# A fused attention and routed feed-forward kernel: another order of work at the start, and three output products behind the last P V

## The chip, the cores and the metric

The kernel runs on one core of one Trainium2 chip. The time is the device time of one execution in microseconds (us), taken as the median of three runs. Five engines work side by side and wait for each other by semaphores: TensorE (in a profile PE, and PEld for its weight loads), VectorE (DVE), ScalarE (ACT), GpSimd (POOL) and SyncE (SP), which here only issues DMAs. Each engine takes its instructions in the order in which they were written.

## The reference: what is computed

With x of 2048 rows and 512 columns, in float32:

```python
g = sigmoid((x * gate_w).sum(-1, keepdims=True))
# a: attention, 32 heads of 16, softmax over all 2048 keys, then wo
q, k, v = split(x @ wqkv)
a = merge(softmax(q @ k.T * 16 ** -0.5) @ v) @ wo
# b: two rows of x, those with the largest r, get a gated feed-forward
r = x @ w_r
idx = argsort(-r)[:2]
y = (silu(x[idx] @ w_gate) * (x[idx] @ w_up)) @ w_down
b = x, with y * sigmoid(r[idx]) added to the rows idx
return g * a + (1 - g) * b
```

## The kernel before, in words

The heads are taken in 16 pairs. A pair has two units of 1024 queries, 32 units in all, and a unit is 16 steps of 128 keys: 512 steps. A step has four score matmuls (`s_piece`, L648) with an exp each on ScalarE (L649) and, two steps later, the P V product (`av_mm`, L657). So that the exp can't overflow, the negative row maxima of the scores are found ahead, by a second product of the same queries and keys (`m_piece`, L576) and a reduction on VectorE (L580). Float32 operands go through TensorE as a high and a low half. `split` makes the halves (high on ScalarE, L70 or L73; low on VectorE, L71 or L74), and the three products of halves are summed. `pool_split` (L77, L78) does the same on GpSimd.

The order is written by hand. `ORDER` (L31) gives the order of pieces for three steps: s is a score piece, m a maximum piece, A a P V, f a piece of other work out of the generator `slots` (projections of the other groups, the feed-forward, the output product with wo). `at_step` hangs small tasks behind a step; `late` holds tasks until the next turn of the loop. Functions in `gaps` are run on VectorE between two reductions.

**The start.** Warm-up products run while weights (`load_w`, L118) and x (`load_x`, L138, four blocks of 512 rows) are loaded. x and the weights of head group 0 are split. `proj` (L146) makes one block of k or q out of twelve products in a PSUM bank (three banks with the tag "st", shared with V's parts and the score pieces). The block is split on leaving the bank; `first_rows` copies its rows for pair 0 into `Kx[0]` or `Qx[0]`, four DMAs a block (L202, L203), and `store_ev` (L176) puts the whole block into DRAM, from where later pairs load it. The blocks leave through two buffers with the tag "ev" (even blocks) or through the tiles Qx[1] and Qx[2] (odd blocks). Before the lead stand k0, q0, k1, k2, k3 and four parts of three products of q1.

**The lead.** `LEAD` is 21 steps of maximum pieces alone (`m_lead`, L607, reduced at L612): 16 for unit 0 and five for unit 1. Between them TensorE takes parts of three products from `lead_parts`: q1, q2, q3, and 64 parts of V (`v_part`, L283), three parts a step, four in the first four steps. Parts that are left come at the first two A of the loop. The first lead step reads blocks 0 and 1 of K, from the fifth on blocks 2 and 3 as well. At the same time the router's and the gate's products of x run on GpSimd (`products`, L315), with their sums on ScalarE (`sums`, L319); the rows of x for them come by `load_rows` (L307, L309). After the last lead step a transpose (`r_row`, L331) turns the router's sums into rows.

**Queues.** All DMAs but the indirect ones are issued by SyncE, in program order. A DMA waits there until the one issued eight before it has landed, and for its data.

**The end.** Once the maxima are done the loop becomes one step at a time: four score pieces, a P V, one piece of `slots`. The last pieces are `wo_last` (L554): the product of head group 3 with wo for one block of 128 rows, three matmuls (L498), added into `acc` on VectorE (`finish`, L549) and stored (`store`, L552). Blocks 8 to 11 come from step 505 on. `tail` (L740) takes the last unit, which covers rows 1536 to 2047: it copies o out of PSUM (L670), sums and inverts the denominators (L746, L748), spreads them (L751, L752, L755), scales o (L758), splits it and makes four output blocks (L765), each finished and stored.

Of the kernel before, what the change touches and what calls it, by code (L numbers as in the profile page):

```python
# [8 lines left out]
F32 = mybir.dt.float32  # L9
# [27 lines left out]
def gated_mix(ctx: ExitStack, tc: tile.TileContext, xT, x, wqkv, wo, w_rg, w_gate, w_up, w_down,  # L37
# [74 lines left out]
    def load_w(g):  # L112
        ws = ring.tile([128, 2, 4, 128], F32, tag="w", name="ws", bufs=3)
        W[g] = ws
        for i in (1, 0):
            if g == 0 and i == 0:
                load_x(0)
            nc.sync.dma_start(ws[:, i], ap(wqkv, i * D + g * 128, [[3 * D, 128], [128 * 3 * D, 4], [1, 128]]))  # L118

    def split_w(g, parts=(1, 0)):  # L120
        if 1 in parts:
# [24 lines left out]
    def proj(g, which, nb, piece):  # L146
        i = "qk".index(which)
        wh, wl = W[g]
        ps = fl_tile() if g else st_tile()
        n = 0  # L150
        for terms in (((wh, xh), (wl, xh)), ((wh, xl),)):
            for c in range(4):
                for a, b in terms:
                    nc.tensor.matmul(ps, a[:, i, c, :], b[nb][:, c, :], start=n == 0, stop=n == 11)  # L154
                    n += 1
                    if n % piece == 0 and n < 12:
                        yield
        if g:
            if (g, which, nb) == (2, "q", 3):
                late.append((split_w, (3, (1,))))  # L160
                at_step(now[0] + 2, split_w, 3, (0,))
            late.append((evict, (g, which, nb, ps)))
            yield
            return
        if nb % 2:
            ev = Qx[1 if nb == 3 else 2].rearrange("p (a n) -> p a n", a=2)
        else:
            ev = ring.tile([128, 2, 512], F32R, tag="ev", name="ev", bufs=2)
        scale = 0.25 if which == "q" else 1.0
        split(ev[:, 0], ev[:, 1], ps, scale=scale)  # L170
        first_rows(which, nb, ev)
        store_ev(0, which, nb, ev)
        yield

    def store_ev(g, which, nb, ev):
        nc.sync.dma_start(  # L176
# [17 lines left out]
    def first_rows(which, nb, ev):  # L194

        if which == "q" and nb > 1:
            return
        t = (Kx if which == "k" else Qx)[0][:, nb * 512:nb * 512 + 512].bitcast(F32)
        for j in range(2):
            e = ev[16 * j:16 * j + 16].bitcast(F32)  # L200
            two = e if which == "k" else e[:, 0:1, :].to_broadcast([16, 2, 512])
            nc.sync.dma_start(t[64 * j:64 * j + 32], two)  # L202
            nc.sync.dma_start(t[64 * j + 32:64 * j + 48], e[:, 0 if which == "k" else 1, :])  # L203

    def proj0(which, nb):
        for _ in proj(0, which, nb, 12):
# [7 lines left out]
    load_w(0)  # L214
    for nb in range(1, 4):
        load_x(nb)
    nc.sync.dma_start(cst, consts)
    wvs = ring.tile([128, 4, 512], F32, tag="P", name="wvs", bufs=3)
    nc.sync.dma_start(wvs, ap(wqkv, 2 * D, [[3 * D, 128], [128 * 3 * D, 4], [1, D]]))
    def ones(k):  # L220
        for j in range(2):
            nc.gpsimd.memset(k[64 * j + 32:64 * j + 64, :].bitcast(F32), 1.0)
# [9 lines left out]
    split_x(2)  # L232
    proj0("q", 0)
    split_x(3)
    for nb in (1, 2, 3):
        proj0("k", nb)
    wv = [wvs, Kx[1].rearrange("p (c n) -> p c n", c=4),
          ring.tile([128, 4, 512], F32R, tag="P", name="wvl", bufs=3)]
    for c in range(4):
# [47 lines left out]
    def lead_parts():  # L287

        v = [(t, c) for t in range(KT) for c in range(4)]
        yield from proj(0, "q", 1, 3)  # L290
        for n in range(8):
            v_part(*v.pop(0))
            yield
        for nb in (2, 3):
            yield from proj(0, "q", nb, 3)
        while v:
            v_part(*v.pop(0))
            yield
# [4 lines left out]
    def load_rows(nb):  # L303
        if nb == 0:
            rg["w"] = o_tile("wr", [128, D]), o_tile("wg", [128, D])
            for i in range(2):
                nc.sync.dma_start(rg["w"][i], ap(w_rg, i * D, [[0, 128], [1, D]]))  # L307
        t = ring.tile([128, 4, D], F32, tag="xs", name="xn", bufs=2)
        nc.sync.dma_start(t, ap(x, nb * 512 * D, [[D, 128], [128 * D, 4], [1, D]]))  # L309
        rg[nb] = t  # L310

# [17 lines left out]
    def r_row():  # L329
        ps = fl_tile((16, 128))  # L330
        nc.tensor.transpose(ps, gz[:, :, 0], ident)  # L331
        rg["row"] = ring.tile([16, 128], F32, tag="rt", name="rt", bufs=1)
        nc.scalar.activation(rg["row"], ps, AF.Copy)

    def route_rows():

# [403 lines left out]
    def tail():  # L740
        u = UNITS - 1
        hl = [o_tile(n, [128, 512], F32R) for n in ("onh", "onl")]
        o = AV[u]
        ps = st_tile((128, 16))
        for c in range(4):
            nc.tensor.matmul(ps[:, 4 * c:4 * c + 4], o[:, c * 128:c * 128 + 128], sel_l, start=True, stop=True)  # L746
        r = ring.tile([128, 16], F32, tag="r16", name="rl", bufs=2)
# [2 lines left out]
        rb = r[:, :, None].to_broadcast([128, 16, 32])  # L750
        nc.scalar.activation(rx[:, 0:8], rb[:, 0:8], AF.Copy)  # L751
        nc.vector.tensor_copy(rx[:, 8:16], rb[:, 8:16])  # L752
        pr = [mxb_tile((128, 256)), fl_tile((128, 256))]
        for c in range(4):
            nc.tensor.matmul(pr[c // 2][:, c % 2 * 128:c % 2 * 128 + 128],  # L755
# [3 lines left out]
        for t in range(2):  # L759
            sl = slice(256 * t, 256 * t + 256)  # L760
            split(hl[0][:, sl], hl[1][:, sl], o[:, sl])
        banks = [st_tile(), mxa_tile()[:, 0], st_tile(), mxb_tile()]
        for t in range(4):
            for n, (a, b) in enumerate(((0, 0), (1, 0), (0, 1))):
                nc.tensor.matmul(banks[t], hl[a][:, t * 128:t * 128 + 128], wz[0][:, b, :], start=n == 0, stop=n == 2)  # L765
# [21 lines left out]
    at_step(1, gates, 0)  # L787
    at_step(2, gaps.append, lambda: nc.vector.max(top8, rg["row"]))
    at_step(3, gaps.append, route_rows)
    at_step(4, gaps.append, partial(gates, 1))  # L790
    at_step(10, gaps.append, lambda: nc.vector.max(best8, cand))
    at_step(12, gaps.append, route_best)
    at_step(18, route_index)
    at_step(22, route_gate, 0)
    at_step(24, gather)
    at_step(27, gaps.append, partial(route_gate, 1))
    at_step(-8, load_w, 1)
    at_step(-5, split_w, 1)
    at_step(2, load_w, 2)
# [11 lines left out]
    def slots():  # L811
# [110 lines left out]

    while count["m"] < UNITS * EL:
        run_late()
        for o in ORDER:
# [60 lines left out]
```

## Time and profile before

| | us |
|---|---|
| median of three runs | 1433.41 (1433.03 to 1433.73) |
| the profiled execution, its own time | 1430.75 |
| its span, first to last instruction | 1428.9 |
| mean granted TensorE clock | 0.999 |

The profile is that of one execution. A row of the timeline gives start, length, engine (SPq is SyncE's issue of a DMA), line, operation and what it writes and reads; in brackets stands how long the engine had been idle and what ended that. PE and PEld overlap, and matmuls are pipelined. A row "x9" merges nine instructions.

### The profile page before, as it was taken

What the parts mean: (1) busy time and instruction counts of PE and PEld (TensorE: products, weight loads), DVE (VectorE), ACT (ScalarE), POOL (GpSimd) and SP (SyncE); (2) the same over time, 40 slices, a digit from 0 to 9 for tenths busy, and PEclk for the clock granted to TensorE, in tenths of its full rate; (3) what the DMA queues carried; (4) which work ended last, traced back from release to release, by engine and by line L of the source; (5) the groups of instructions that cost most, each with busy time, mean ns of one, the idle gap of its engine ahead of it and who ended that gap; (6) DMA issues with size and microseconds to landing.
All of it is one profiled execution on the core that took longest, in us unless ns stands there. A gap on an engine that the chain in (4) does not pass through costs nothing.

```text
span 1428.9 us, 24152 instructions
## 1 busy us (share of the span) xinstructions
PE 1417.6 (99%) x9113; PEld 628.9 (44%) x9113; DVE 1292.6 (90%) x1534; ACT 1169.4 (82%) x2262; POOL 312.9 (22%) x329
## 2 busy tenths in 40 slices
PE   9999999999999999999999999999999999999998
PEld 6654444444444444444444443434444444444433
DVE  5879999999999999999999999999999999999942
ACT  4468888888888888888888888888888888888886
POOL 3661100112000001200000100032742322234500
PEclk9999999999999999999999999999999999999999
DMA  8611021212214121312222332414313031012012
GB/s 261 183 56 49 20 53 31 54 45 43 53 52 109 62 53 31 68 29 57 65 82 53 85 84 77 106 41 134 83 31 68 21 77 35 15 31 58 17 50 78
DMA packets 55096, 92.87 MB, mean 65 GB/s; under 512 B 14208, under 2 KB 25472, under 8 KB 53476
## 3 DMA queue, kind: packets, MB, share of 16 engines
q1 hardware_dynamic: 54884, 91.32, 24.7%
q8 instruction: 72, 1.18, 0.4%
q14 instruction: 44, 0.36, 0.1%
q0 software_dynamic: 96, 0.01, 0.0%
HBM read 63.77 MB, written 28.57 MB: 65 GB/s over the span
## 4 chain that ended last, share of the span: by engine, by line
PE 97%; DMA 2%; SPq 0%; DVE 0%; ACT 0%; issue 0%; ACTq 0%; DVEq 0%
PE av L657 36%; PE st L648 24%; PE mxa L576 12%; PE mxb L576 10%; PE fl L154 6%; PE fl L498 4%; PE st L283 3%; DMA xs<-xT 1%; PE mxa L607 1%; DMA wvs<-wqkv 1%; PE fl L389 0%; PE st L154 0%; DMA k_scr<-Qx 0%; PE fl L427 0%; ACT P L649 0%; DVE acc L549 0%
## 5 line engine op out<-in xcount | busy, mean ns | idle before, releaser
L649 ACT ACTIVATE P<-st 128x512 f32<-128x512 f32 x2028 | 1064.4, 599 | 200.7 <-PE st L648 108.8
L580 DVE TENSOR_REDUCE Mr<-mxa 128x2 f32<-128x1024 f32 x655 | 796.6, 1216 | 3.9 <-PE mxa L576 3.0
L657 PE MATMUL av<-P,V 128*32 128x512 f32 x4096 | 545.3, 605 | 0.0
L648 PE MATMUL st<-Qx,Kx 50*128 50x512 f32 x2028 | 537.5, 443 | 1.8 <-ACT P L649 1.8
L580 DVE TENSOR_REDUCE Mr<-mxb 128x1 f32<-128x512 f32 x654 | 450.9, 689 | 62.6 <-PE st L648 20.6
L648 PEld LDWEIGHTS st<-Qx,Kx 50*128 50x128 f32 x2028 | 276.7, 184 | 232.3 <-ACT P L649 213.4
L576 PE MATMUL mxb<-Kx,Qx 48*128 48x512 f32 x654 | 325.3, 497 | 0.0
L576 PE MATMUL mxa<-Kx,Qx 48*128 48x512 f32 x1310 | 296.0, 418 | 0.0
L576 PEld LDWEIGHTS mxb<-Kx,Qx 48*128 48x128 f32 x654 | 119.5, 183 | 273.7 <-DVE Mr L580 271.2
L576 PEld LDWEIGHTS mxa<-Kx,Qx 48*128 48x128 f32 x1310 | 124.9, 183 | 46.5 <-DVE Mr L580 5.4
L657 PEld LDWEIGHTS av<-P,V 128*32 128x32 f32 x4096 | 81.1, 108 | 141.5 <-issue 135.3
L77 POOL TENSOR_SCALAR hl<-m 128x16 fp32r<-128x16 f32 x32 | 8.1, 255 | 434.3 <-DVE m L623 434.3
L190 POOL TENSOR_SCALAR ev<-pe 128x512 fp32r<-128x512 f32 x24 | 35.8, 1492 | 299.0 <-ACT pe L188 299.0
L465 POOL TENSOR_TENSOR acc<-acc,w 128x512 f32<-128x512 f32 x32 | 41.0, 1281 | 166.7 <-ACT w L464 152.4
L154 PE MATMUL fl<-xh,wh 128*128 128x512 f32 x96 | 42.9, 447 | 0.0
L154 PE MATMUL fl<-xh,wl 128*128 128x512 f32 x96 | 40.4, 421 | 0.0
L549 DVE SCALAR_TENSOR_TENSOR acc<-fl,gg,acc 128x512 f32<-128x512 f32 x16 | 12.0, 748 | 26.3 <-PE fl L498 24.1
L498 PE MATMUL fl<-woh,ahl 128*128 128x512 f32 x96 | 35.1, 447 | 0.0
L612 DVE TENSOR_REDUCE Mr<-mxa 128x2 f32<-128x1024 f32 x21 | 25.7, 1223 | 8.2 <-PE mxa L607 8.2
L154 PE MATMUL fl<-xl,wh 128*128 128x512 f32 x96 | 32.6, 420 | 0.0
L191 POOL TENSOR_TENSOR ev<-pe,ev 128x512 fp32r<-128x512 f32 x24 | 30.9, 1286 | 2.0
L319 ACT ACTIVATE p<-p 128x512 f32<-128x512 f32 x32 | 20.0, 628 | 11.1 <-POOL p L315 10.9
(173 smaller groups left out, 765.0 us busy)
## 6 DMA issues: line engine op xcount, KB each, us to landing
Kx<-k_scr SPq DMA_DIRECT2D x30, 256.0 KB
k_scr<-ev SPq DMA_DIRECT2D x14, 512.0 KB
q_scr<-ev SPq DMA_DIRECT2D x14, 512.0 KB
Qx<-q_scr SPq DMA_DIRECT2D x54, 128.0 KB
Qx<-q_scr SPq DMA_DIRECT2D x70, 64.0 KB
xs<-xT SPq DMA_DIRECT2D x16, 256.0 KB
xn<-x SPq DMA_DIRECT2D x4, 1024.0 KB
Qx<-hr SPq DMA_DIRECT2D x256, 2.0 KB
```

The costliest lines, as they stand in the source:

```text
L154: nc.tensor.matmul(ps, a[:, i, c, :], b[nb][:, c, :], start=n == 0, stop=n == 11)
L190: nc.gpsimd.tensor_scalar(ev[:, 0], t, 1.0, None, op0=OP.mult)
L191: nc.gpsimd.tensor_sub(ev[:, 1], t, ev[:, 0].bitcast(F32))
L283: nc.tensor.matmul(ps, a[nb][:, c, sl], b[:, c, :], start=c == 0 and n == 0, stop=c == 3 and n == 2)
L465: nc.gpsimd.tensor_add(a, a, w)
L498: nc.tensor.matmul(ps, a[:, sl], b[:a.shape[0], c, :], start=first and n == 0, stop=last and n == 2)
L576: nc.tensor.matmul(dst, Qx[u % 3][64 * j:64 * j + 48, t * 128:t * 128 + 128], k_of(u, t // 4)[64 * j:64 * j + 48, c * 512:c * 512 + 512], ...
L580: nc.vector.tensor_reduce(Mr[:, g0:g0 + (2 if r == 1 else 1)], MX[r - 1], axis=AX.X, op=OP.max, negate=True)
L612: nc.vector.tensor_reduce(*r, axis=AX.X, op=OP.max, negate=True)
L648: nc.tensor.matmul(ps, k, q, start=True, stop=True)
L649: nc.scalar.activation(P[s][:, 2 * j + c, :], ps, AF.Exp)
L657: nc.tensor.matmul(AV[0][32 * ct:32 * ct + 32, :], V[:, kt, h * VW:h * VW + 32], P[s][:, ct, :], start=kt == 0, stop=kt == KT - 1)
```

## The change

What it does, part by part:

- The weights lie in DRAM in another order, made on the host: the columns of a group of q or k as rows of 512 values, and V's weights as rows of 2048. The loads carry the same bytes.
- The start: k0, q0, k1 as before, then V's weights are split, then k2, k3, q1, q2 whole. The lead begins behind them, takes four parts of q3 in its first step and V's parts after. The constants are loaded behind the last of these projections.
- Blocks k1, k2 and k3, q1 leave through two larger buffers with the tag "xs" (where blocks 0 and 1 of x had been); k0, q0, q2 and q3 through the two "ev" buffers.
- The stores into DRAM are held in a list: k0 and q0 are stored behind the copies of k1, the next five behind the router's first row loads (issued with q2), q3 alone.
- For k1, k3 and q1 the two copies of the second head are issued by GpSimd's queue instead of SyncE's.
- The router's x rows 0 and 1 go into buffers with the tag "P", 2 and 3 into "xs". `products` starts a step later, so that one pair is ahead of `sums` instead of two. The eviction of the router's row goes into `late`. Its best, index and gather steps come two steps later.
- For unit 0, the split of the maxima is made on VectorE (the high half by a reduction straight into the rounded type).
- `slots` ends with row block 8. Blocks 9, 10 and 11 are made in `tail`: 10 behind the last P V (finished on VectorE), 11 behind the sums of the denominators and 9 behind the spread (both added through ScalarE and GpSimd). Their stores stand ahead of the last four in SyncE's queue.

```diff
-            nc.sync.dma_start(ws[:, i], ap(wqkv, i * D + g * 128, [[3 * D, 128], [128 * 3 * D, 4], [1, 128]]))
+            nc.sync.dma_start(ws[:, i], ap(wqkv, (2 * g + i) * 128 * D, [[D, 128], [128, 4], [1, 128]]))
...
-        if nb % 2:
-            ev = Qx[1 if nb == 3 else 2].rearrange("p (a n) -> p a n", a=2)
-        else:
-            ev = ring.tile([128, 2, 512], F32R, tag="ev", name="ev", bufs=2)
+        ev = ev0(which, nb)
         scale = 0.25 if which == "q" else 1.0
         split(ev[:, 0], ev[:, 1], ps, scale=scale)
         first_rows(which, nb, ev)
-        store_ev(0, which, nb, ev)
+        scr.append((0, which, nb, ev))
+        if (which, nb) in (("k", 1), ("q", 2), ("q", 3)):
+            if nb == 2:
+                load_rows(0)
+                load_rows(1)
+            for e in scr[:2] if nb == 1 else scr:
+                store_ev(*e)
+            del scr[:2 if nb == 1 else 9]
         yield
+
+    scr, evs = [], []
+
+    def ev0(which, nb):
+        if (which, nb) in (("k", 1), ("k", 3)):
+            t = ring.tile([128, 2, 2, 512], F32R, tag="xs", name="evx", bufs=2)
+            evs.extend([t[:, 0], t[:, 1]])
+        if evs:
+            return evs.pop(0)
+        return ring.tile([128, 2, 512], F32R, tag="ev", name="ev", bufs=2)
...
-            nc.sync.dma_start(t[64 * j:64 * j + 32], two)
-            nc.sync.dma_start(t[64 * j + 32:64 * j + 48], e[:, 0 if which == "k" else 1, :])
+            queue = nc.gpsimd if j and (which, nb) in (("k", 1), ("k", 3), ("q", 1)) else nc.sync
+            queue.dma_start(t[64 * j:64 * j + 32], two)
+            queue.dma_start(t[64 * j + 32:64 * j + 48], e[:, 0 if which == "k" else 1, :])
...
-    nc.sync.dma_start(cst, consts)
...
-    nc.sync.dma_start(wvs, ap(wqkv, 2 * D, [[3 * D, 128], [128 * 3 * D, 4], [1, D]]))
+    nc.sync.dma_start(wvs, ap(wqkv, 8 * 128 * D, [[4 * D, 128], [D, 4], [1, D]]))
...
-    for nb in (1, 2, 3):
-        proj0("k", nb)
+    proj0("k", 1)
...
-        yield from proj(0, "q", 1, 3)
-        for n in range(8):
-            v_part(*v.pop(0))
-            yield
-        for nb in (2, 3):
-            yield from proj(0, "q", nb, 3)
+        yield from proj(0, "q", 3, 3)
...
-        t = ring.tile([128, 4, D], F32, tag="xs", name="xn", bufs=2)
+        t = ring.tile([128, 4, D], F32, tag="P" if nb < 2 else "xs", name="xn", bufs=3 if nb < 2 else 2)
...
-    nc.scalar.activation(rg["row"], ps, AF.Copy)
+    late.append((nc.scalar.activation, (rg["row"], ps, AF.Copy)))
...
-        pool_split(hl[:, :, 0], hl[:, :, 1], m)
+        if u == 0:
+            nc.vector.tensor_reduce(hl[:, :, 0], Mr[:, 0:EL].rearrange("p (t c j) -> p j t c", c=4, j=2), axis=AX.X, op=OP.min)
+            nc.vector.tensor_sub(hl[:, :, 1], m, hl[:, :, 0].bitcast(F32))
+        else:
+            pool_split(hl[:, :, 0], hl[:, :, 1], m)
...
+        pw = mxa_tile()
+        pw = pw[:, 0], pw[:, 1], st_tile()
+        def late_wo(i):
+            wo_terms(pw[i], *lastp[1], 3, slice((2 + i if i < 2 else 1) * 128, (3 + i if i < 2 else 2) * 128), True, True)
+        late_wo(0)
+        finish(10, pw[0])
+        store(10)
         for c in range(4):
             nc.tensor.matmul(ps[:, 4 * c:4 * c + 4], o[:, c * 128:c * 128 + 128], sel_l, start=True, stop=True)
...
+        late_wo(1)
+        acc_add(11, pw[1], gg)
+        store(11)
         pr = [mxb_tile((128, 256)), fl_tile((128, 256))]
...
+        late_wo(2)
+        acc_add(9, pw[2], gg)
+        store(9)
-        banks = [st_tile(), mxa_tile()[:, 0], st_tile(), mxb_tile()]
+        banks = [st_tile(), av_tile(), st_tile(), mxb_tile()]
...
-    for nb in range(4):
-        at_step(-20 + 4 * nb, load_rows, nb)
+    at_step(-13, load_rows, 2)
+    at_step(-9, load_rows, 3)
...
-        at_step(-19 + t, products, t)
+        at_step(-18 + t, products, t)
...
-        for t in range(12):
+        for t in range(9):
...
-    parts_next(4)
+    for w, nb in (("k", 2), ("k", 3), ("q", 1), ("q", 2)):
+        proj0(w, nb)
+    nc.sync.dma_start(cst, consts)
...
-        parts_next(3 + (s < -LEAD + 4))
+        parts_next(3 + (s == -LEAD))
...
-                    parts_next(3)
+                    parts_next(2)
```

More of the change, by code (lines that the diff above doesn't have):

```diff
@@ L784, in gated_mix @@
     for t in range(16):
-        at_step(-19 + t, products, t)
+        at_step(-18 + t, products, t)
     at_step(-1, r_row)
-    at_step(1, gates, 0)
     at_step(2, gaps.append, lambda: nc.vector.max(top8, rg["row"]))
     at_step(3, gaps.append, route_rows)
+    at_step(1, gates, 0)
     at_step(4, gaps.append, partial(gates, 1))
-    at_step(10, gaps.append, lambda: nc.vector.max(best8, cand))
-    at_step(12, gaps.append, route_best)
-    at_step(18, route_index)
+    at_step(12, gaps.append, lambda: nc.vector.max(best8, cand))
+    at_step(14, gaps.append, route_best)
     at_step(22, route_gate, 0)
-    at_step(24, gather)
     at_step(27, gaps.append, partial(route_gate, 1))
+    at_step(20, route_index)
+    at_step(26, gather)
     at_step(-8, load_w, 1)
@@ L970 @@
     consts[:, 134] = 128 * p
+    w = np.asarray(inputs["A_wqkv"]).reshape(4, 128, 3, 4, 128)
+    wqkv = np.concatenate([w[:, :, :2].transpose(3, 2, 1, 0, 4).ravel(), w[:, :, 2].transpose(1, 0, 2, 3).ravel()])
     arrays = {
-        "xT": np.ascontiguousarray(x.T), "x": x, "wqkv": np.ascontiguousarray(inputs["A_wqkv"]),
+        "xT": np.ascontiguousarray(x.T), "x": x, "wqkv": wqkv,
         "wo": np.ascontiguousarray(inputs["A_wo"]),
```

## The prediction

> **What bounds the kernel now.** I read the page first, then the busy times by stretch (columns: length, busy time of PE, PEld, DVE, ACT and POOL with their instructions, granted clock, DMA share, GB/s), then the order of time at the two ends of the run, where alone work is moved.
>
> ```profile
> span 1428.9 us, 24152 instructions
> PE 1417.6 (99%) x9113; PEld 628.9 (44%) x9113; DVE 1292.6 (90%) x1534; ACT 1169.4 (82%) x2262; POOL 312.9 (22%) x329
> ...
> PE 97%; DMA 2%; SPq 0%; DVE 0%; ACT 0%; issue 0%; ACTq 0%; DVEq 0%
> ```
>
> ```profile
> 24.00:27.00 3.00, 1.29 (x6) 0.51 (x4) 2.85 (x4) 2.01 (x4) 1.90 (x2) 0.96 0.85 205
> 27.00:31.00 4.00, 4.00 (x12) 2.90 (x12) 0.80 (x3) 0.60 (x1) 1.16 (x1) 0.61 0.60 132
> 45.00:93.00 48.00, 48.00 (x214) 31.56 (x213) 40.82 (x53) 29.19 (x78) 42.99 (x36) 1.00 0.45 139
> 135.00:535.00 400.00, 400.00 (x2642) 173.13 (x2642) 379.96 (x441) 335.88 (x645) 45.52 (x50) 1.00 0.22 54
> ```
>
> The chain that ended last is TensorE for 97%. In the loop (135 to 535 us) TensorE is never free and VectorE is busy 95%; the order of TensorE's work there stays. What can be won lies where TensorE stands still: at the start of the lead and after the last P V. Between 24 and 27 us it is busy 1.29 of 3.00, and over the next 4 us its granted clock is 0.61. The order of time says why:
>
> ```profile
> 22.74 0.59 SPq L202 DMA_DIRECT2D Kx<-Qx  x1
> 24.29 0.50 PE L607 MATMUL mxa<-Kx,Qx 48*128 48x512 f32 x2
> 26.50 0.55 PE L607 MATMUL fl<-Kx,Qx 48*128 48x512 f32 x1 [1.71 <-DMA Kx<-Qx]
> 29.61 0.60 ACT L73 ACTIVATE Qx<-st 128x512 fp32r<-128x512 f32 x1 [3.60 <-DMA k_scr<-Qx]
> 32.12 0.50 PE L607 MATMUL mxa<-Kx,Qx 48*128 48x512 f32 x2 [0.32 <-DVE Mr L612]
> 36.07 0.50 PE L607 MATMUL mxa<-Kx,Qx 48*128 48x512 f32 x2
> 39.69 0.50 PE L607 MATMUL mxa<-Kx,Qx 48*128 48x512 f32 x2
> ```
>
> ```profile
> 44.03 2.27 PE st L283 x9
> 90.98 2.27 PE st L283 x9
> ```
>
> The first four lead steps begin at 24.29, 32.12, 36.07 and 39.69. A step with twelve part products takes 39.69 - 36.07 = 3.62 when nothing is late, so the third could have begun at 24.29 + 2 x 3.62 = 31.53; it began 4.54 late. Block 1 of K is in Kx only at 26.50, its copies having stood in SyncE's queue until 22.74 behind stores and copies of earlier blocks; ScalarE waits 3.60 for a store to free a buffer, VectorE behind it reduces late, and the clock falls to half for a while. From the fifth step (parts at 44.03) to the last (90.98), a step takes 46.95 / 16 = 2.93.
>
> **The copies ahead of the stores, seven projections before the lead, K blocks in other buffers.** No product is removed.
>
> ```profile
> 3.82 0.63 ACT L70 ACTIVATE wh<-ws 128x512 fp32r<-128x512 f32 x1 [1.81 <-DMA ws<-wqkv]
> 18.26 1.70 POOL L71 TENSOR_TENSOR xl<-xs,xh 128x512 fp32r<-128x512 f32 x1 [1.21 <-ACT xh L70]
> 18.73 0.68 DVE L74 SCALAR_TENSOR_TENSOR Qx<-st,Qx 128x512 fp32r<-128x512 f32 x1
> 18.76 0.39 PE L154 MATMUL st<-xh,wh 128*128 128x512 f32 x1
> 20.79 0.59 SPq L202 DMA_DIRECT2D Qx<-ev  x1
> 21.48 0.39 PE L154 MATMUL st<-xh,wh 128*128 128x512 f32 x1
> 23.82 2.19 ACT L70 ACTIVATE Kx<-wvs 128x512 fp32r<-128x512 f32 x4
> 47.95 1.29 POOL L315 TENSOR_TENSOR p<-xn,wr 128x512 f32<-128x512 f32 x1 [19.79 <-DMA xn<-x]
> 93.09 0.27 PE L331 MATMUL fl<-cst,gz 128*16 128x128 f32 x1
> 94.47 0.50 PE L648 MATMUL st<-Qx,Kx 50*128 50x512 f32 x1 [0.68 <-ACT P L649]
> ```
>
> ```profile
> L350 POOL DMA_INDIRECT idx<-i_scr,pos x1: 1063/1063/1063, 138.3 to 138.3; - x1
> ```
>
> Before the lead stand seven projections, where six products' worth (five blocks and the four early parts of q1) stood; one takes 21.48 - 18.76 = 2.72. The lead then begins at 24.29 + 2.72 = 27.0, its second step at 30.6, and twenty steps of 2.93 end at 89.3. Before, they ended at 93.09 with the router's transpose: 3.8 less. One V part fewer is left for the loop's first round, three products of the nine that take 2.27 with their drain: 0.7. **-4.5**, the whole stall.
>
> For this the first step's copies must be in by 27. Block 1 is split as before at 18.73 + 0.68 = 19.4, SyncE reaches its first copies there (no store ahead), so two land some 3 us earlier than 26.50. The other two go through POOL's queue, free at 18.26 + 1.70 = 19.96. No direct copy from that queue is in the trace; the indirect one held POOL for 1.06. Two of them: 22.1, and the landing within zero and double the 3.76 (22.74 to 26.50) that the SyncE copies took. I take the 3.76, the nearest row: 25.9, a margin of 1.1 us; the far end gives rival A. The split of block 2 now stands behind the split of V's weights on ScalarE, which needs their load; rival B. The router's rows are loaded some 10 us sooner and POOL's chain of products (42.99 of 48 us, from 47.95) starts sooner than it did, so it hides as before; SyncE's later entries (rows, q loads, the eight hr copies) meet no wait that the lead does not outlast by 4 us.
>
> Smaller: the weight loads come in 2 KB rows, four times fewer. ScalarE waited 1.81 for the first. Between 0 and 0.8 won; I take **-0.3**. The router's row is evicted at the same place of ScalarE's order, and its step wins nothing. In the first round TensorE waited 0.68 for an exp to free a bank; there the V part that closes now is whole, and between 0 and 0.7 goes: **-0.3**. The first unit's row split on VectorE costs two instructions of about 0.2 us in 2.93 us steps with 40.82 of 48 us busy: nothing; without that room, 0.4. The router's later steps and gathers move by two steps and touch no path: nothing, or 0.3 either way.
>
> **The three products behind the last P V.**
>
> ```profile
> 1407.57:1410.14 2.57, 2.57 (x17) 0.94 (x15) 0.75 (x2) 2.07 (x5) 0.00 (x0) 1.00 0.27 102
> 1410.14:1412.07 1.93, 1.93 (x13) 0.54 (x11) 0.32 (x1) 1.93 (x5) 0.00 (x0) 1.00 0.35 136
> 1412.07:1414.22 2.15, 2.15 (x14) 0.64 (x13) 0.00 (x0) 2.10 (x6) 0.00 (x0) 1.00 0.03 8
> 1424.50:1427.60 3.10, 0.60 (x3) 0.18 (x1) 1.39 (x3) 0.00 (x0) 0.00 (x0) 1.00 0.90 338
> ```
>
> ```profile
> 1408.70 0.74 PE L498 MATMUL fl<-woh,lahl 128*128 128x512 f32 x2
> 1409.60 0.73 PE L648 MATMUL st<-Qx,Kx 50*128 50x512 f32 x3
> 1418.14 1.06 PE L746 MATMUL st<-cst,o 128*128 128x4 f32 x8 [0.72 <-ACT o L670]
> 1420.06 0.71 PE L755 MATMUL mxb<-cst,rxl 128*128 128x128 f32 x4 [0.86 <-ACT rxl L751]
> 1421.85 0.50 PE L765 MATMUL st<-wz,onh 128*128 128x512 f32 x1 [0.63 <-ACT onh L70]
> ```
>
> ```profile
> 1423.85 2.40 SPq L552 DMA_DIRECT2D out<-acc  x4
> ```
>
> ```profile
> L465 POOL TENSOR_TENSOR acc<-acc,w 128x512 f32<-128x512 f32 x32 | 41.0, 1281 | 166.7 <-ACT w L464 152.4
> ```
>
> ```profile
> L465 POOL TENSOR_TENSOR acc<-acc,w 128x512 f32<-128x512 f32 x32 | 41.0, 1281 | 166.7 <-ACT w L464 152.4
> ```
>
> A late step with a product takes 2.57, one without 2.15 (ScalarE busy 2.10 of it), the one between 1.93. Three fewer with it: 3 x (2.57 - 2.15) = **-1.2**. In the tail a product holds TensorE from 1408.70 to 1409.60, 0.9; the three gaps are 0.72, 0.86 and 0.63, so the last matmuls start 0.5 later, of which 0.3 is taken up where they waited for VectorE: 0.2. The end, though, is a store. Four stores of 256 KB were issued from 1423.85 and kept the DMA engines busy at 0.90 until 1427.6, 0.71 each (2.85 from the first data). Now row block 9's stands before them, and it waits for the third product (about 1422.45), ScalarE's 0.6 (as at 29.61), POOL's 1.28: issue at 1424.45 instead of 1423.85, then five stores instead of four: 0.6 + 0.7 = **+1.3**. If its add comes early the cost falls to 0.2, if it meets VectorE's work it reaches 2.0.
>
> **Sum.** -4.5 - 0.3 - 0.3 - 1.2 + 1.3 = -5.0. The profiled execution took 1430.75 us (span 1428.9 and 1.85 around it): 1425.75. The median of the three runs, 1433.41, lies 2.66 above it; I put the same difference on it: **1428.4 us**. Its own range is -6.9 to -3.7 with the bounds above: 1426.5 to 1429.7.
>
> **Rivals.** A, the copies through POOL's queue land late: at double the landing, 22.1 + 7.5 = 29.6, TensorE stands 2.1 and, as at 27 to 31 us, loses half of some 3.4 us of clock, 1.7: 3.8 back, 1432.2. For it: no such copy is in the trace. Against it: 1.1 us of margin. The Trainium skill, SBUF — State Buffer, Who interferes with whom, speaks of this: writing descriptors for POOL's queue is held up while VectorE runs a two-port instruction, and a tensor_tensor isn't one. VectorE runs no other SBUF-only work there, so by that rule there is no delay and A falls; no row here shows it.
>
> The clock's part in A has a row: 1.71 us of standing still, in a stretch 1.29 of 3.00 busy, and 0.61 granted after it. The Trainium skill, TensorE: Matmul & The Clock Gate, What's actually happening, asks for about 3.4 us of idling before the clock halves; the stall here was shorter, so row and rule differ. By the rule A would cost 2.1 and end at 1430.5; I keep the row.
>
> B, V's weights come late: ScalarE waits for them with block 2's eviction behind it, and q2 needs that bank at about 21.48 + 2.72 = 24.2, a little less for its first product. The load was in by 20.79 (SyncE then went on); V's split (2.19), block 2's eviction (0.6) and its lower half (0.68) add 3.5, so 20.5 is the limit. It is issued 0.7 sooner and no store runs beside it: about 19. In by 22 it would cost 1.5 and 1.7 of clock: 1431.6.
>
> C, the other side: the loop falls into another rhythm. From 93.29 (0.20 behind the transpose) to 1409.60 are 509 steps, 7.76 for a round of three; with VectorE at 95% little decides who waits. 0.06 more in each of 164 rounds is +9.8: 1438.2. It decides from 0.05 (+7.9, slower by 0.2%). For it: the start shifts every queue. Against it: TensorE's order in the loop is the same, and nothing new waits there.
>
> **How the numbers follow.** 0.2% (2.9 us) is about what a measurement of this kernel tells from no change: faster is below 1430.5, slower above 1436.3. Forecast 0.68, A 0.09, B 0.10, C 0.13. Faster: the forecast and part of B, 0.72; same: A, the rest of B and a mild C, 0.14; slower 0.14. The range takes in A and B: 1426.2 to 1432.2, and leaves out C.
>
> **What would show it.** Right: the lead's first group at about 27 with the clock at full share from 24 to 31, its last step ending near 89, no wait of TensorE on a copy of Kx; late steps of 2.15; block 9's store before the last four, which end as late after the last P V as +1.3 says. Wrong: TensorE waiting for Kx (A) or for a bank held by block 2 (B) between 23 and 31; a round of the loop above 7.8; output stores that end over 2 us later behind the last P V.

## The result, and the profile after

| | before | after |
|---|---|---|
| median | 1433.31 us (6 runs, 1431.57 to 1433.73) | 1425.82 us (6 runs, 1424.97 to 1426.95) |
| the profiled execution | 1430.75 us, span 1428.9 | 1426.34 us, span 1424.4 |

The ratio is 0.9951, with a 95% interval of 0.9941 to 0.9961: by it the change makes the kernel 0.49% faster, 7.0 us, and the two medians lie 7.5 us apart. The forecast was 1428.4, with a range of 1426.2 to 1432.2. The median of 1425.82 lies 0.4 below that range; 0.9951 of the median that the prediction started from (1433.41) is 1426.4, just inside it. So the way and the rough size were right, and the gain was larger than forecast. The two profiles explain only 4.5 us of the 7.5; where the other 3 come from is the first question below.

The page of the changed kernel (span; busy time of the engines; the chain that ended last, by engine):

```profile
span 1424.4 us, 24160 instructions
...
PE 1416.3 (99%) x9113; PEld 627.8 (44%) x9113; DVE 1292.2 (91%) x1534; ACT 1169.2 (82%) x2264; POOL 318.5 (22%) x335
...
PE 99%; DMA 0%; ACT 0%; DVE 0%; SPq 0%; issue 0%; DVEq 0%; ACTq 0%
```

Its busy times by stretch, columns as in the prediction, and below them its order of time on TensorE:

```profile
24.00:27.00 3.00, 3.00 (x13) 2.17 (x13) 1.89 (x4) 0.64 (x2) 2.66 (x4) 1.00 1.13 270
27.00:31.00 4.00, 4.00 (x19) 2.69 (x18) 2.65 (x4) 0.60 (x1) 0.54 (x2) 1.00 0.90 179
...
1398.19:1408.31 10.12, 10.12 (x61) 3.21 (x59) 0.33 (x1) 10.04 (x21) 0.00 (x0) 1.00 0.07 26
```

```profile
27.61 0.50 PE L617 MATMUL mxa<-Kx,Qx 48*128 48x512 f32 x2
...
31.22 0.50 PE L617 MATMUL mxa<-Kx,Qx 48*128 48x512 f32 x2
...
89.81 0.27 PE L341 MATMUL fl<-cst,gz 128*16 128x128 f32 x1
...
1408.88 2.78 PE L671 MATMUL av<-P,V 128*32 128x512 f32 x24
...
1419.25 0.39 PE L794 MATMUL mxb<-wz,onh 128*128 128x512 f32 x1
```

Where TensorE was busy 1.29 of 3.00 us it is now busy all of it, and the granted clock from 27 to 31 us is 1.00 where it was 0.61. The lead's first two steps begin at 27.61 and 31.22, the router's transpose stands at 89.81 instead of 93.09, five late steps take 10.12 (2.02 each), and the last group of P V products begins at 1408.88 instead of 1414.65. The stores end 4.8 us behind the last matmul (1424.4 against 1419.64), where it was 3.8.

### The profile page after: what moved, and what is told of

Read it like the earlier page. It is cut to its first block, busy times and chain, and to the rows that moved or that the text cites. A ratio compares the mean times of both kernels' runs of the same rounds, so it can differ in the third digit from the quotient of the medians.

```text
span 1424.4 us, 24160 instructions
## 1 busy us (share of the span) xinstructions
PE 1416.3 (99%) x9113; PEld 627.8 (44%) x9113; DVE 1292.2 (91%) x1534; ACT 1169.2 (82%) x2264; POOL 318.5 (22%) x335
## 4 chain that ended last, share of the span: by engine, by line
PE 99%; DMA 0%; ACT 0%; DVE 0%; SPq 0%; issue 0%; DVEq 0%; ACTq 0%
PE av L671 36%; PE st L662 24%; PE mxa L586 12%; PE mxb L586 10%; PE fl L154 6%; PE fl L508 4%; PE st L298 3%; PE st L154 2%; PE mxa L617 1%; PE fl L399 1%; DMA xs<-xT 0%; PE fl L437 0%; PE mxb L662 0%; DVE acc L559 0%; ACT P L663 0%; PE mxa L508 0%
## 5 line engine op out<-in xcount | busy, mean ns | idle before, releaser
L300 ACT ACTIVATE V<-st 128x512 f32<-128x512 f32 x16 | 9.6, 600 | 27.7 <-PE st L298 27.7
```

## Experiment 1: where the rest of the 7.5 us is

In the prediction the profiled execution's distance to the median, 2.66 us, was carried over unchanged. It wasn't the same for both kernels: the changed one's profiled execution lies 0.5 above its median. So the kernel before seems to lose something in most of its executions that its one profile doesn't show. The first run is that kernel once more.

> The kernel before, unchanged, for more executions with their spans and clocks. The profiled execution of before took 1430.75 us, its other runs 1431.6 to 1433.7; after a change that the two profiles put at 4.5 us, the medians differ by 7.5. Theory H: the 3 us between are in the start of the kernel before, where the clock fell to half for 3.4 us in the profiled execution; in other executions it stays there for twice that or the stall is longer. Then these spans lie about 1.7 to 3 us above 1428.9, the mean clock of the long ones is 0.998 instead of 0.999, and a second profile shows more than 4.5 us lost before the third lead step. Rival O: the time around the span varies. Then the spans stay at 1428.9 and the times spread by 2 to 3 us.

Measured: 1433.36 (1432.43 to 1435.29), ratio 0.9995 (0.9986 to 1.0004); span of the profiled execution 1431.8, 2.9 longer than the first one's. Its order of time at the end, and the busy times of one stretch there:

```profile
1415.32 2.78 PE L657 MATMUL av<-P,V 128*32 128x512 f32 x24
1418.82 1.05 PE L746 MATMUL st<-cst,o 128*128 128x4 f32 x8 [0.72 <-ACT o L670]
1420.73 1.23 PE L755 MATMUL mxb<-cst,rxl 128*128 128x128 f32 x4 [0.86 <-ACT rxl L751]
...
1423.03 0.79 PE L765 MATMUL st<-wz,onh 128*128 128x512 f32 x1 [0.23 <-ACT onh L70]
...
1427.63 0.39 PE L765 MATMUL mxb<-wz,onh 128*128 128x512 f32 x1
```

```profile
1421.00:1425.00 4.00, 3.77 (x12) 2.95 (x13) 1.69 (x5) 0.83 (x2) 0.00 (x0) 0.50 0.00 0
```

The same stretch, the last P V and the last product of the first profile of that kernel:

```profile
1421.00:1425.00 4.00, 3.37 (x14) 2.20 (x13) 3.36 (x7) 0.74 (x2) 0.00 (x0) 1.00 0.08 29
...
1414.65 2.78 PE L657 MATMUL av<-P,V 128*32 128x512 f32 x24
...
1424.71 0.39 PE L765 MATMUL mxb<-wz,onh 128*128 128x512 f32 x1
```

Theory H had the longer spans right and the place wrong: the loss is at the end, not at the start. Rival O falls, since the span itself is longer. From the last P V to the end of the last product this execution needs 1428.02 - 1415.32 = 12.70 us, the first profile's 1425.10 - 1414.65 = 10.45: 2.25 more, at a granted clock of 0.50. The waits are those of the first profile (0.72 and 0.86); what differs is whether the clock falls behind them. The remaining 0.7 comes from the lead (transpose at 93.77 instead of 93.09).

The mean granted clock is on record for executions without a profile too. A mean of 0.996 over 1430 us stands for some 11 us at half clock (0.004 x 1430 / 0.5, an estimate); the second profile has 3.41 in the lead and 6.83 in the tail. Of the 63 executions of the kernel before that ran beside other kernels here, 43 show 0.996 or less; of the ten of this run three do. The clock isn't all of the spread: one of these ten has 0.999 and a span of 1432.1.

With this second execution as "before", the difference adds up by stage:

| stage | forecast | first profiles | second profile of before, to after |
|---|---|---|---|
| to the router's transpose | -4.1 | -3.3 | -4.0 |
| transpose to last P V (first rounds, loop, late steps) | -2.2 | -2.5 | -2.5 |
| last P V to the end of the last product | +0.2 | +0.3 | **-1.9** |
| from there to the end of the stores | +1.1 | +1.0 | +1.0 |
| sum | -5.0 | -4.5 | -7.4 |

(The forecast's first line is 3.8 of the stall and 0.3 for the start, its second the V part, the wait for a bank and the late steps.) Is it the cover in the tail that makes the third line negative? The two halves of the change alone, and the change with two products in the tail instead of three:

```diff
 head_only (the changed kernel): tail() and the twelve wo_last as before
-        for t in range(9):
+        for t in range(12):
 tail_only (the kernel before): the changed tail() and
-        for t in range(12):
+        for t in range(9):
 two_tail (the changed kernel): no late_wo(2), block 9 made in the late steps
-        for t in range(9):
+        for t in range(10):
```

> The changed kernel with the tail and the twelve late products of before. By the two traces the three products won 1.5 us in the late steps and cost 1.3 behind the last P V, so this should be 0.2 us slower than the changed kernel (1425.8), within what can be measured. Rival: the tail carries the part of the gain that the two profiles do not explain; then it is 2 to 3 us slower than the changed kernel.

> The kernel before with only the three products put behind the last P V. By the traces 1.5 won and 1.3 lost: 0.2 us faster than before, no difference that can be measured. By the rival above 2 to 3 us faster.

> The changed kernel with block 9 back in the late steps, so that only blocks 10 and 11 are made behind the last P V. If the end is set by five stores in a row behind GpSimd's late add, the end comes 0.6 + 0.7 us earlier for one late step that is 0.4 longer: about 0.9 us faster than the changed kernel. If the stores do not set the end, it is 0.4 slower.

| run | median | ratio to before (95%) |
|---|---|---|
| the kernel before, same chip | 1434.28 | |
| head_only | 1428.83 | 0.9963 (0.9950 to 0.9977) |
| tail_only | 1431.38 | 0.9986 (0.9977 to 0.9995) |
| two_tail | 1426.46 | 0.9946 (0.9933 to 0.9960) |

head_only and tail_only came out as their rivals say. The tail, for which the prediction had +0.1 (-1.2 and +1.3), is worth 2.9 us by the medians when it alone is changed (2.0 by the ratio, 0.7 to 3.3 by its interval), and head_only, without it, lies 2.4 over two_tail. In head_only the old waits are back, and the products behind them stand 0.43 apart instead of 0.23:

```profile
1418.11 0.79 PE L779 MATMUL st<-wz,onh 128*128 128x512 f32 x1 [0.63 <-ACT onh L70]
...
1420.01 0.63 PE L779 MATMUL mxa<-wz,onl 128*128 128x512 f32 x1
1420.44 0.63 PE L779 MATMUL mxa<-wz,onh 128*128 128x512 f32 x1
```

two_tail gains as much as the whole change (0.9946 against 0.9951), neither 0.9 faster nor 0.4 slower: the third product, whose store the prediction charged with most of +1.3, costs and brings nothing that these runs can tell. Its late step comes back (last P V at 1409.72), and the stores end sooner behind the last product (4.2 us instead of 4.8).

Moved work and covered waits go together in these runs. To part them, the kernel before got cover only, products whose result nobody reads:

```diff
+        pw = mxa_tile()
+        def cover():
+            for _ in range(3):
+                nc.tensor.matmul(pw[:, 1], wz[0][:, 0, :128], wz[0][:, 0, :], start=True, stop=True)
 ...
+        cover()      # ahead of the sums, of the spread, and of the four output blocks
```

> The kernel before with nothing moved; in each of the three waits of the last unit's normalisation TensorE gets three products of 128 x 512 whose result nobody reads, so the sums are the same. Theory H (the waits of the old tail, 1.31, 1.11 and 0.91 us between products, drop the granted clock in most executions and cost 2.25 us there, which the one profile of before did not show): 1.0 to 2.6 us faster than before by the median, clock 1.00 up to the last product. Rival (what the three real products gain is their work taken out of the late steps): no change, 0 to 0.3 us slower.

(The rows of before put the three waits at 0.72, 0.86 and 0.63 us.) Measured: 1431.63 (11 runs) beside 1433.66, ratio 0.9988 (0.9979 to 0.9997): with nothing moved 2.0 faster by the medians, 1.7 by the ratio, 0.4 to 3.0 by its interval. The last product starts 10.06 behind the last P V, to the hundredth what the first profile of before has at full clock (1424.71 - 1414.65):

```profile
1415.66 2.78 PE L657 MATMUL av<-P,V 128*32 128x512 f32 x24
1418.37 0.96 PE L749 MATMUL mxa<-wz 128*128 128x512 f32 x3
...
1425.72 0.39 PE L774 MATMUL mxb<-wz,onh 128*128 128x512 f32 x1
```

Each wait here is under a microsecond, and no store depends on the added products. None of the 11 executions shows a mean clock of 0.996 or less. That settles it: the tail's gain is the clock that its waits used to take away. Of the 7.5 us it is about 2.

## Experiment 2: what took the stall of the lead away

The prediction named two things: K's copies ahead of the stores (block 1 in Kx by 26 instead of 26.5) and a seventh projection that covers the time until then. The rows of before name a third thing: q1's eviction waits on ScalarE for a store that frees its buffer (3.60 us, until 29.61). Two runs, each with one half:

```diff
 order_only (the changed kernel)
-    for w, nb in (("k", 2), ("k", 3), ("q", 1), ("q", 2)):
+    for w, nb in (("k", 2), ("k", 3), ("q", 1)):
 (q2 in the lead's steps, stores behind q1's copies, five steps with a part more)
 cover_only (the kernel before)
+        yield from proj(0, "q", 2, 3)        # in lead_parts, ahead of V's parts
-    parts_next(4)
+    parts_next(8)
-        parts_next(3 + (s < -LEAD + 4))
+        parts_next(3)
```

> The changed kernel, unchanged, beside the other three on one chip. Both theories: 1425.8 us, 7.5 to 8.5 under the kernel before; lead's first group at 27.6, router's transpose at 89.8, last group of 24 P V products at 1408.9. It is the number that the next two are held against.

> The changed kernel, but q's third projection goes back into the lead's steps, so that the lead begins behind six projections, as before, with the copies of K's rows and the stores in the changed order (all stores behind q1's copies, and the evictions in buffers that wait for no store). Theory O (the order of stores, copies and buffers is what took the stall away): lead's first group at 24.7, a wait of at most 1.0 us for block 1 of K on TensorE, second step at 28.4 without a wait for VectorE, and with five steps of one part more the router's transpose at 89.7 to 90.7; time 0 to 1.0 us over the changed kernel. Theory C (the cover by the seventh projection took it away): a wait of 2 us or more on TensorE in the first step, half clock behind it, the transpose at 92 to 93, time 2 to 3.5 us over the changed kernel.

> The kernel before, but with q's third projection whole ahead of the lead (seven projections ahead of it, as in the changed kernel) and three parts in each step of the lead; stores, copies and buffers as before. Theory C: the lead begins at 27.0, no wait on TensorE, second step at 30.6, router's transpose at 89.3 to 90: 3 to 4 us faster than before. Theory O: q1's eviction still waits on ScalarE for the store of k1 whose buffer it takes over (29.6 in the profile before), its lower half stands in VectorE's queue ahead of the first step's reductions (30.2), q2's stands there too, so that the second step waits for VectorE until 32.5 to 33.5 and the transpose comes at 91 to 92: 1 to 2 us faster than before.

| run | median | ratio to before (95%) | lead's steps 1, 2, 3 begin | router's transpose |
|---|---|---|---|---|
| the kernel before, same chip | 1433.66 | | 24.29, 32.12, 36.07 (first profile) | 93.09 |
| the changed kernel | 1426.45 | 0.9950 (0.9935 to 0.9966) | 27.92, 31.53, 34.46 | 90.14 |
| order_only | 1426.40 | 0.9947 (0.9932 to 0.9962) | 25.18, 29.62, 33.23 | 90.92 |
| cover_only | 1434.19 | 1.0003 (0.9994 to 1.0012) | 27.36, 33.16, 37.78 | 93.43 |

The changed kernel itself came out 7.2 us under the kernel before, a little less than expected. Without the seventh projection it is as fast as with it, as theory O says, and TensorE waits for no copy of K. Its lead begins 0.5 later than theory O had it, though, TensorE then waits 0.76 for a bank, and its transpose lies 0.2 outside the range. The seventh projection alone brings nothing, less than both theories gave it. In cover_only the first step no longer waits for K, and the second waits for VectorE instead (ScalarE, VectorE, TensorE):

```profile
30.05 0.60 ACT L73 ACTIVATE Qx<-st 128x512 fp32r<-128x512 f32 x1 [3.87 <-DMA Kx<-ev]
...
30.68 0.69 DVE L74 SCALAR_TENSOR_TENSOR Qx<-st,Qx 128x512 fp32r<-128x512 f32 x1 [3.44 <-ACT Qx L73]
31.29 0.68 DVE L74 SCALAR_TENSOR_TENSOR ev<-st,ev 128x512 fp32r<-128x512 f32 x1
31.89 1.22 DVE L612 TENSOR_REDUCE Mr<-mxa 128x2 f32<-128x1024 f32 x1
```

```profile
33.16 0.68 PE L607 MATMUL mxa<-Kx,Qx 48*128 48x512 f32 x2 [2.80 <-DVE Mr L612]
```

q1's high half is written at 30.05, into the buffer of k1, once a DMA has let go of it (the profile names a copy here, and the store of k1 in the kernel before); its low half and q2's stand on VectorE ahead of the first step's reductions. TensorE waits 2.80, and half clock follows (33.32 to 36.73), as theory O's wait for VectorE has it. So the wait for K was not what set the second step. The next runs ask whether the half clock in the lead of before was, and whether the buffers were:

```diff
 lead_fill (the kernel before), ahead of the lead's first step
+    fb = mxb_tile()
+    for _ in range(9):
+        nc.tensor.matmul(fb, W[0][0][:, 0, 0, :], xh[0][:, 0, :], start=True, stop=True)
 cover_buf (cover_only), the buffers of the changed kernel
-        if nb % 2:
-            ev = Qx[1 if nb == 3 else 2].rearrange("p (a n) -> p a n", a=2)
-        else:
-            ev = ring.tile([128, 2, 512], F32R, tag="ev", name="ev", bufs=2)
+        if (which, nb) in (("k", 1), ("k", 3)):
+            t = ring.tile([128, 2, 2, 512], F32R, tag="xs", name="evx", bufs=2)
+            evs.extend([t[:, 0], t[:, 1]])
+        ev = evs.pop(0) if evs else ring.tile([128, 2, 512], F32R, tag="ev", name="ev", bufs=2)
```

> The kernel before with nine products of 128 x 512 ahead of the lead's first step whose result nobody reads; they stand where TensorE waited 2.2 us for block 1 of K. It prices the half clock by itself. Theory B: TensorE runs at full clock from 24 to 30, but the second step still begins at 32.1 to 33, because VectorE's reductions of the first stand behind q1's eviction; the half clock cost nothing there, and the time is that of before, within 0.5 us. Rival (the half clock cost 1.7 us of the stall): second step at 30.5 to 31, transpose 1.5 us sooner than in the kernel before, 1.2 to 1.7 us faster.

> As the kernel with the seventh projection ahead of the lead, and besides the blocks k1, k2 and k3, q1 leave through the two larger buffers of the changed kernel, so that no eviction waits for a store; every store and copy stands in SyncE's queue where it stood before the change. Theory B (what held the second step was the buffer: q1's eviction behind k1's store, with VectorE's reductions behind it; the copies' place in the queue is hidden by the seventh projection): lead's first group at 27.4, second step at 31.0 without a wait for VectorE, clock full from 24 to 40, router's transpose at 89.7 to 90.5; 3 to 4 us faster than before (1429.5 to 1430.5). Rival (the copies ahead of the stores are needed as well): TensorE waits 1 us or more for a copy of K or a later step does for VectorE, transpose at 91.5 or later; less than 2 us faster.

Measured beside 1433.29 for the kernel before: lead_fill 1433.77, ratio 1.0002 (0.9993 to 1.0011); cover_buf 1432.69, ratio 0.9995 (0.9986 to 1.0004). The order of time in lead_fill:

```profile
24.46 2.20 PE L916 MATMUL mxb<-xh,wh 128*128 128x512 f32 x9
26.59 0.50 PE L607 MATMUL mxa<-Kx,Qx 48*128 48x512 f32 x2
...
32.99 0.51 PE L607 MATMUL mxa<-Kx,Qx 48*128 48x512 f32 x2 [1.74 <-DVE Mr L612]
...
38.54 0.50 PE L607 MATMUL mxa<-Kx,Qx 48*128 48x512 f32 x2
```

(The wait that these nine fill is 1.71 us in the row of before; they take 2.20.) The clock is full from 24 to 31, and the second step begins about where it did, at 32.99 (32.12 and 32.76 in the two profiles of before), behind q1's eviction (30.48). The time is as theory B had it. But the half clock did not go: it came behind the new wait, from 34.01 to 37.42, and the third step follows after 5.55 instead of 3.95. In this execution the transpose even stands at 95.55, 2.5 later than in the first profile of before. So this run shows that the first half clock did not set the second step, and doesn't price a lead without half clock.

cover_buf was theory B's own test, and B falls short. Its first two steps are those of the changed kernel (27.69 and 31.04, no wait), and yet the transpose stands at 93.78. What its rival named did come (a later wait for VectorE, the transpose after 91.5), but not for the rival's reason: TensorE waits for no copy of K. The time is lost again fifty microseconds on. The order of time on GpSimd, VectorE and TensorE:

```profile
81.22 0.25 POOL L77 TENSOR_SCALAR hl<-m 128x16 fp32r<-128x16 f32 x1
...
90.51 1.29 POOL L317 TENSOR_TENSOR p<-xn,wg 128x512 f32<-128x512 f32 x1
```

```profile
81.80 0.21 DVE L636 STREAM_TRANSPOSE hr<-hl 128x32 f32<-128x32 f32 x1 [3.47 <-POOL hl L78]
81.94 1.18 DVE L614 TENSOR_REDUCE Mr<-mxa 128x2 f32<-128x1024 f32 x1
```

```profile
83.18 0.50 PE L609 MATMUL mxa<-Kx,Qx 48*128 48x512 f32 x2 [1.89 <-DVE Mr L614]
```

With the lead sooner, the split of unit 0's maxima still stood in GpSimd's queue behind the router's products, which begin at 48.71 (x's rows land late) and fill it. VectorE waits 3.47 for it with reductions behind, TensorE 1.89, and half clock follows (85.11 to 88.52). In the changed kernel the split is VectorE's own, and the products begin at 39.07 and end earlier. VectorE and GpSimd there:

```profile
75.44 0.21 DVE L637 TENSOR_REDUCE hl<-Mr 128x16 fp32r<-128x64 f32 x1
...
78.14 0.20 DVE L648 STREAM_TRANSPOSE hr<-hl 128x32 f32<-128x32 f32 x1
```

```profile
86.95 1.29 POOL L325 TENSOR_TENSOR p<-xn,wg 128x512 f32<-128x512 f32 x1
```

GpSimd's last product ends at 88.2 in the changed kernel and at 91.8 in cover_buf (90.51 and 1.29), and the router's last sum (0.81) and the transpose come after it. So in cover_buf the transpose could not have come before 92.6 even without the wait at 83.18. These last two steps, the split on VectorE and the earlier load of x's rows, are read off the two traces; no run did either alone. Nor did any run only put the copies ahead of the stores, or take GpSimd's queue out of the changed kernel.

## A version that is faster still

Two small delays were left: block 2's eviction behind the split of V's weights (rival B's mechanism, 0.4 us of TensorE), and row block 9's add on ScalarE and GpSimd.

```diff
 best (the changed kernel)
     proj0("k", 1)
+    proj0("k", 2)
     wv = [...]
-    for w, nb in (("k", 2), ("k", 3), ("q", 1), ("q", 2)):
+    for w, nb in (("k", 3), ("q", 1), ("q", 2)):
 ...
-        acc_add(9, pw[2], gg)
+        finish(9, pw[2])
```

> The changed kernel, but V's weights are split behind the third projection of k instead of the second (so that block 2's eviction on ScalarE doesn't wait for their load), and row block 9 is added by VectorE behind the split of o instead of by ScalarE and GpSimd. The first: no wait of TensorE for a bank ahead of q2, where 0.4 to 0.6 us stood: -0.3 to -0.6. The second: its store goes out at 17.9 in place of 18.4 on the tail's clock (1400 and so much), so the stores end 0.4 us sooner, unless the four last blocks on VectorE, each 0.26 later, set the end: -0.4 to +0.3. Together 0.2 to 1.0 us faster than the changed kernel.

> The changed kernel again, as the measure for the run above: 1425.5 to 1426.7 us.

Measured: 1425.12 (1424.53 to 1425.21, 5 runs), ratio to before 0.9940 (0.9926 to 0.9954), beside 1426.10 (1425.97 to 1427.90, 5 runs) for the changed kernel: 1.0 faster, and the two sets of runs don't overlap. ScalarE in this kernel:

```profile
18.93 0.60 ACT L73 ACTIVATE evx<-st 128x512 fp32r<-128x512 f32 x1 [0.63 <-PE st L154]
20.48 2.20 ACT L70 ACTIVATE Kx<-wvs 128x512 fp32r<-128x512 f32 x4 [0.95 <-DMA wvs<-wqkv]
22.58 0.58 ACT L73 ACTIVATE evx<-st 128x512 fp32r<-128x512 f32 x1
```

Block 2 leaves its bank at 18.93, where in the first profile of the changed kernel it left at 22.97. The stores end 4.2 behind the last product instead of 4.8. How much each of the two brings isn't parted.

## Why the prediction was right, and where it wasn't

**The stall (-4.5).** The size held (-3.3 from the first profile, -4.0 from the second, to the transpose), the reason only in part. "The copies ahead, seven projections before the lead" reads as cover and copies; order_only shows that the seventh projection was not needed, and cover_only that it brings nothing alone. The prediction had the row that mattered, ScalarE's 3.60 us for a store and VectorE reducing late behind it, but put no price on it. What the runs show is that the change without the seventh projection removes the stall, and that this projection with the new buffers does not. The rest of the chain is read off the traces: copies soon enough, and in the lead's second half the split of unit 0's maxima on VectorE. That last one stood in the prediction as "nothing". By the wait of 3.47 us in cover_buf it is one of the conditions for the head's gain.

One reading of the prediction was wrong. It had SyncE reach the copies of k1 at 19.4, with no store ahead of them. In the changed kernel SyncE issued the first of them at 21.47, because it stood 2.1 us on a copy ahead of them, until V's weights had landed, the DMA issued eight before that copy. In the kernel before it had stood 1.8 for the same load. The waits of SyncE between 12 and 90 us and its rows:

```profile
SPq L219 <- DMA wvs<-wqkv: 2.1, 1, 2.1
```

```profile
18.18 0.59 SPq L218 DMA_DIRECT2D Qx<-ev  x1
20.87 0.51 SPq L219 DMA_DIRECT2D Qx<-ev  x1
21.47 0.59 SPq L218 DMA_DIRECT2D Kx<-evx  x1
```

So the new order brought SyncE's first copy of k1 forward by 1.3 us (21.47 instead of 22.74). The two copies in GpSimd's queue went out at 20.09 and 20.84.

**The router's chain.** "It hides as before" was right in the outcome. But in the kernel before it hid with little to spare: its last product ended at 91.1 and its sums at 92.2, 0.9 us ahead of the transpose. GpSimd and ScalarE there:

```profile
89.82 1.28 POOL L315 TENSOR_TENSOR p<-xn,wg 128x512 f32<-128x512 f32 x1
...
91.99 0.19 ACT L319 ACTIVATION_READ_ACCUMULATOR p<-p 128x1 f32 x1
```

By cover_buf's bound of 92.6, a lead that ends 3 us sooner needs a router that ends sooner too; the earlier rows of x were part of the price, not a side effect.

**The start (-0.3)** did not come: the first product stands at 6.60 instead of 6.52, behind the warm-up products. When the lead begins varies from one execution to the next: the same code began it at 27.39 to 27.92 in four profiles, three of the changed kernel and one of two_tail. TensorE's wait for the first halves of x, 0.6 to 1.0 us in these, varies too; whether that is the reason isn't shown.

**Late steps and first rounds (-1.2, -0.3 and the -0.7 of the V part)** together were -2.2 and measured -2.5. A late step without a product takes 2.02 instead of the 2.15 assumed.

**The tail (+1.3)** was right for an execution at full clock: +0.3 and +1.0. Its rows, 0.72, 0.86 and 0.63, were read as time that could hold a product. They were also waits that let the clock fall, and the same prediction had used this for the lead ("1.71 us of standing still ... and 0.61 granted after it") and not asked it here.

**The offset (+2.66) was the step that failed.** "I put the same difference on it" carried over as noise what was mostly half clock in the tail, which the change itself removes. Without the offset the sum gives 1425.75, and the median is 1425.82. That agreement is partly luck. Between the first two profiles the change brought 4.5, not 5.0: to the transpose 3.3 where stall and start had 4.1, against 0.3 more than forecast behind it. And the changed kernel's median lies 0.5 below its profiled execution. That the first profile was of an execution without the tail's loss was chance as well.

**Rivals.** A: no wait of TensorE on a copy of Kx. GpSimd's queue took 0.50 to 0.75 us for each direct copy, less than the 1.06 assumed. The 3.76 us that the prediction took for a landing is no measured one: four copies of k1 went out between 22.74 and 24.71, and TensorE's wait ended at 26.50 with whichever came last. In the changed kernel the copies of K's rows through GpSimd's queue landed 4.1 us after their issue (median). B: its mechanism is there in small. V's weights were split from 20.87, block 2 was evicted at 22.97, and TensorE waited 0.4 for a bank (its weight load in the first profile, its product in the second); the run above takes it away. C: between transpose and last P V the kernel gained 2.5, so the loop lost nothing like 0.06 a round.

**The clock's rule.** The Trainium skill, TensorE: Matmul & The Clock Gate, What's actually happening, says that a free-running window of 3.41 us decides, and that the clock halves after an idle one. The traces agree with the window: in all fourteen profiles every half-clock stretch that ended within the run lasts 3.41 or 6.83 us, and in each they begin on one grid (26.74 and 1429.62 in the first profile of before are 411 windows apart, 27.62 and 1420.26 in the second 408). They don't agree with the idle one: 1.5 us of waiting in a window was enough in the lead (tail_only) and 1.1 to 1.6 in the tail. By the rule the tail's waits would have cost nothing, and the change would have brought some 5 us (7.5 less the 2.25 of the tail, an estimate). Where the grid falls changes from one execution to the next, and so does whether the tail's waits cost anything; that the one decides the other is likely but not shown.

## What to carry to other kernels

A wait that ends last hides the next one: before pricing a stall, follow each engine in it to what it would wait for next (here K's copies, then a buffer held by a store, then a split in GpSimd's queue, then the router's sums). Cutting the first, or the first two, brought nothing that could be told from noise, and all together 3.3 to 4.0 to the transpose. Where the profiled execution lies away from the median, look for the cause in a second profile of the same kernel before carrying the difference over; it may be the very thing that the change removes. Short waits of TensorE that add up to a microsecond or more within 3.4 us can be worth covering even with products that nobody reads, if more products follow: here nine of them saved about 2 us.

## What the runs showed of the hardware

- The granted clock fell to half around waits of 0.72 and 0.86 us in the tail (1420.26 to 1427.09, second profile of before) and cost 2.25 us there; in the first profile the same waits, at another place of the 3.41 us grid, cost nothing.
- What share of a window must be idle isn't settled: 1.3 us in one window of the tail left the clock full in the first profile, while in the second a window with 1.1 us was followed by half clock; in head_only it was 1.4. These figures count a matmul as busy for its modelled length, and the tail's small products may count for less.
- A direct copy through GpSimd's queue held GpSimd 0.50 to 0.75 us and landed 4.1 us after its issue for K's rows and 5.6 for q1's (medians). No landing of a copy through SyncE's queue was measured beside it.
